# Three score products fewer in a pair's shared tile, and reciprocals carried through a scratch row

## The chip, the cores and the metric

The kernel runs on one core of a Trainium2 chip. The metric is device time of one launch in microseconds (us). TensorE (PE) multiplies matrices and transposes, VectorE (DVE) and ScalarE (ACT) read the products from PSUM, GpSimd (POOL) works on SBUF alone, and SyncE (SP) issues the transfers. Each engine runs its instructions in the order in which the program gives them; they meet by semaphores. There is no scheduler: the kernel's Python code writes the order out by hand.

## The reference

16 heads of attention, then two feed-forward layers:

```python
q_pool = q.reshape(B, H, S // 2, 2, D).mean(axis=3)        # 576 queries of 64 in a head
scores = scale * np.matmul(q_pool, k.transpose(0, 1, 3, 2))  # 576 x 1152
scores = scores - np.max(scores, axis=-1, keepdims=True)
attn = np.exp(scores)
attn = attn / (np.sum(attn, axis=-1, keepdims=True) + 1e-09)
out = np.matmul(attn, v)
...
x = moe(x, w_in, w_out)           # ELU between two products
x = moe2(x, w_gate, w_val, w_out, rms_g)   # RMS norm, SiLU gate, product
```

With B = 2, H = 8, S = 1152, D = 64 there are 16 heads. Everything is float32.

## The kernel before, in words

**Precision.** Products run in a rounded float32 format. A matrix is split into a rounded part (hi) and what the rounding left (lo), and a product is the sum of hi x hi, hi x lo and lo x hi. For scores, `kd` holds the keys' hi in partitions 0 to 63 and their lo in 64 to 127 (`prep_k`). `qt` holds the queries' hi twice, in both halves (u = 0), and their lo (u = 1). One stationary block of queries times `kd` sums 128 partitions at once: hi x hi and hi x lo with u = 0, lo x hi (and lo x lo) with u = 1.

**Pairs and tiles.** Heads go in 8 pairs p; j = 0, 1 is the head within a pair. A head's 576 queries are four tiles of 128 and a rest of 64. The two rests share the ninth tile, M (`i == M`, index 2): the stationary block of each head is padded with zero columns, so that rows 0 to 63 of the result come from one head and rows 64 to 127 from the other. For all other tiles a score tile of 128 x 1152 takes 6 matmuls of 384 columns (2 parts x 3 banks, line 350); M takes 4 parts, so 12.

**Steps.** The attention runs in 72 steps, 9 a pair. Here S0 to S8 name the step by its place in its pair. In a step TensorE does the scores of this tile (`emit_S`), 9 transposes of the exponentials of the tile two steps back (`emit_T`, line 368; LT = 2), and about 8 products with the values (`do_AV`, line 394). In between, VectorE scales the scores, takes the row extremum (line 354), and forms the lo parts of the transposes (line 70); ScalarE does the exponential (line 359) and the hi parts (line 376). A score tile's three banks exist once, so the next scores wait for line 354. The transposes rotate over three banks. Before `emit_T` overwrites a buffer of transposes, `do_T` makes TensorE finish the value products that still read it. In pair 0 the tiles come in the order 0, 1, 3, 4, M, 5, 6, 7, 8 and M is S4; in the other pairs they come in the order of their indices and M is S2.

**Preparation.** GpSimd splits queries, keys and values for the next pair, one job a step, by the table `plan`; `prep_q`, `prep_k` and `prep_v` do it. In pair 0 the first head's jobs are spread over three engines, and head j = 0's queries are prepared by GpSimd in two column ranges, 512 to 576 first (these are M's), then 0 to 512. SP loads the raw arrays one job ahead (`fetch`).

**Row sums.** After a pair's last tile, `emit_r` takes 1/(row sum + 1e-9) for the 9 tiles, a 128 x 9 array, and GpSimd spreads 8 of its columns to 512. `emit_scale` transposes this by 4 matmuls in S6 of the next pair (line 433) and the ninth column by one in S7 (line 438), ScalarE copies them into `xs` (lines 435, 441), and `emit_x` multiplies the pair's output by `xs` on GpSimd. In steps where this is due, the transposes of `emit_T` come behind the value products. The last pair (p = 7) has its own, quicker ending on VectorE and ScalarE.

After attention come the two feed-forward layers, which the change doesn't touch.

Of the kernel before, what the change touches and what calls it, by code (L numbers as in the profile page):

```python
# [39 lines left out]
def tile_kernel(ctx: ExitStack, tc: tile.TileContext, qd, kd, vd, w1d, w2d, wgd, wvd, wod, rgd, outd):  # L40
# [377 lines left out]
    def emit_r(p):  # L418
        s = st[p]
        V.tensor_scalar(out=s[:, 2], in0=s[:, 1], scalar1=1e-9, scalar2=None, op0=ALU.add)  # L420
        V.reciprocal(s[:, 3], s[:, 2])
        rs[p] = ap.tile([128, 640], F32, tag="xs", name="rs", bufs=1)[:, 0:512].rearrange("p (a b) -> p a b", a=8)
        hi_pool(rs[p], s[:, 3, 0:8].to_broadcast([128, 8, 64]))
# [63 lines left out]
    plan = {1: lambda p: ("v", p, 0), 2: lambda p: ("q", p + 1, 1), 3: lambda p: ("k", p + 1, 1, 0),  # L487
            4: lambda p: ("k", p + 1, 1, 1), 5: lambda p: ("v", p + 1, 1), 6: lambda p: ("q", p + 1, 0),
            7: lambda p: ("k", p + 1, 0, 0), 8: lambda p: ("k", p + 1, 0, 1)}
    steps = [(p, i) for p in range(8) for i in ([0, 1, 3, 4, 2, 5, 6, 7, 8] if p == 0 else range(NPT))]  # L490
    ns = len(steps)
    jobs = {n: [] for n in range(-1, ns)}
    for n in range(ns):
# [4 lines left out]
        if k in plan and not (p == 0 and k == 1):  # L498
# [81 lines left out]
    for step in range(ns):  # L580
        emit_S(*steps[step])
# [6 lines left out]
        if step >= LT and not due:  # L588
# [6 lines left out]
        if step >= LT and due:  # L595
            do_T(step)
# [507 lines left out]
```

## Time and profile before

| what | value |
|---|---|
| time of three runs | 667.54, 668.39, 668.79 us; median 668.39 us |
| profiled execution, first to last instruction (span) | 666.8 us |
| the profiled execution's own time | not given with the profile; the median of the runs is 1.6 us over its span |
| TensorE busy | 659.0 us, 99% of the span |
| attention | about the first 250 us |
| VectorE, ScalarE, GpSimd busy over the span | 511.5, 465.2, 443.6 us |
| granted TensorE clock | full in all 40 slices |

Busy shares are means over stages. In attention three engines stand near their limit at once, so the stage is read pair by pair and step by step, with what each engine waits for. Matmuls overlap in the records: the time that one adds is the distance between starts, or its piece in the chain of waits, not its duration.

### The profile page before, as it was taken

Reading aid. Unit: us, or ns where it says so; the run is one execution under the profiler, and the core shown is the slowest. Engines: PE = TensorE matmul, PEld = TensorE weight load, DVE = VectorE, ACT = ScalarE, POOL = GpSimd, SP = SyncE. Lnnn points to the kernel's source line nnn. Section 1 sums busy time; section 2 is a strip of 40 time slices with the busy share of each in tenths; the row PEclk is TensorE's granted clock in tenths of the full one; section 3 lists DMA queues with packets and bytes.
Section 4 is the critical chain, followed back from the end, with each engine's and each line's share of the span. In section 5 each row is a group of like instructions: output and inputs, shape, how many; then the busy total and the mean of one; then the engine's idle time right before and its main releaser. Section 6 shows DMA issues by size and latency. Waiting matters only on the chain.

```text
span 666.8 us, 11391 instructions
## 1 busy us (share of the span) xinstructions
PE 659.0 (99%) x4149; PEld 652.1 (98%) x4149; DVE 511.5 (77%) x884; ACT 465.2 (70%) x910; POOL 443.6 (67%) x407
## 2 busy tenths in 40 slices
PE   7999999999999999999999999999999999999997
PEld 6999999999999999999999999999999999999997
DVE  7989898998999878987786787688697786676200
ACT  6988888898988977848758668866766654564300
POOL 4999888989989323758776695665998874404200
PEclk9999999999999999999999999999999999999999
DMA  6432333233223101142141232110323322204100
GB/s 177 171 107 90 108 131 133 90 108 121 90 89 94 46 1 64 43 148 95 64 158 65 94 129 94 65 64 32 126 96 125 129 94 68 91 1 162 68 36 36
DMA packets 21624, 61.75 MB, mean 93 GB/s; under 512 B 2752, under 2 KB 5056, under 8 KB 21568
## 3 DMA queue, kind: packets, MB, share of 16 engines
q1 hardware_dynamic: 21568, 61.03, 27.9%
q8 instruction: 32, 0.52, 0.3%
q14 instruction: 24, 0.20, 0.1%
HBM read 58.66 MB, written 2.36 MB: 92 GB/s over the span
## 4 chain that ended last, share of the span: by engine, by line
PE 96%; POOL 1%; DVE 1%; DMA 1%; issue 0%; SPq 0%; ACT 0%; POOLq 0%; ACTq 0%
PE b L747 17%; PE b L217 14%; PE b L219 14%; PE b L218 14%; PE s L350 12%; PE o L394 11%; PE t L368 10%; DMA rawq<-in_q_dram 1%; PE t L433 1%; DVE p L354 0%; POOL kd L64 0%; POOL qt L64 0%; PE fb L217 0%; PE fb L219 0%; PE fb L218 0%
## 5 line engine op out<-in xcount | busy, mean ns | idle before, releaser
L64 POOL TENSOR_TENSOR wl<-wt,wh 128x512 fp32r<-128x512 f32 x68 | 91.1, 1340 | 83.9 <-ACT wh L184 79.0
L70 DVE TENSOR_TENSOR ptl<-t,pth 128x384 fp32r<-128x384 f32 x216 | 106.7, 549 | 4.9 <-ACT pth L376 4.5
L354 DVE TENSOR_SCALAR_CACHE_REDUCE p<-s 128x1152 f32<-128x1152 f32 x72 | 97.4, 1354 | 15.1 <-PE s L350 13.7
L376 ACT CAST pth<-t 128x384 fp32r<-128x384 f32 x216 | 89.2, 488 | 22.3 <-PE t L368 21.6
L350 PE MATMUL s<-kd,qt 128*128 128x384 f32 x480 | 98.7, 342 | 2.9 <-DVE p L354 1.4
L359 ACT ACTIVATE p<-p,st 128x1152 f32<-128x1152 f32 x72 | 91.5, 1271 | 0.5 <-DVE p L354 0.2
L217 PE MATMUL b<-xh,wh 128*128 128x384 f32 x260 | 87.7, 337 | 0.0
L350 PEld LDWEIGHTS s<-kd,qt 128*128 128x128 f32 x480 | 81.0, 188 | 6.6 <-DVE p L354 2.8
L219 PE MATMUL b<-xh,wl 128*128 128x384 f32 x260 | 87.5, 336 | 0.0
L218 PE MATMUL b<-xl,wh 128*128 128x384 f32 x260 | 87.4, 336 | 0.0
L394 PE MATMUL o<-pth,vd 128*128 128x256 f32 (+1 forms) x288 | 84.4, 315 | 0.0
L368 PE MATMUL t<-ident,p 128*128 128x128 f32 x648 | 82.5, 272 | 0.0
L394 PE MATMUL o<-ptl,vd 128*128 128x256 f32 (+1 forms) x288 | 78.6, 295 | 0.0
L368 PEld LDWEIGHTS t<-ident,p 128*128 128x128 f32 x648 | 75.0, 141 | 1.8
L120 ACT ACTIVATE we<-wr 128x512 uint32<-128x512 uint32 x68 | 45.4, 667 | 38.8 <-DMA wr<-in_w_dram 19.1
L131 DVE TENSOR_SCALAR wm<-wm 128x512 f32<-128x512 f32 x63 | 43.8, 695 | 20.3 <-ACT wm L122 20.3
L394 PEld LDWEIGHTS o<-pth,vd 128*128 128x128 f32 x288 | 54.3, 189 | 0.3
L122 ACT ACTIVATE wm<-wr 128x512 f32<-128x512 f32 x63 | 39.6, 628 | 21.4 <-DVE wt L136 21.3
L394 PEld LDWEIGHTS o<-ptl,vd 128*128 128x128 f32 x288 | 54.5, 189 | 0.0
L218 PEld LDWEIGHTS b<-xl,wh 128*128 128x128 f32 x260 | 48.8, 188 | 0.0
L217 PEld LDWEIGHTS b<-xh,wh 128*128 128x128 f32 x260 | 48.8, 188 | 0.0
L219 PEld LDWEIGHTS b<-xh,wl 128*128 128x128 f32 x260 | 48.8, 188 | 0.0
(198 smaller groups left out, 1750.6 us busy)
## 6 DMA issues: line engine op xcount, KB each, us to landing
wr<-in_w_dram SPq DMA_DIRECT2D x32, 512.0 KB, 3.2
rawq<-in_q_dram SPq DMA_DIRECT2D x15, 576.0 KB, 4.0
rawk<-in_k_dram SPq DMA_DIRECT2D x28, 288.0 KB, 2.9
wr<-in_wg_dram SPq DMA_DIRECT2D x12, 512.0 KB, 3.2
wr<-in_wv_dram SPq DMA_DIRECT2D x12, 512.0 KB, 3.2
wr<-in_wo_dram SPq DMA_DIRECT2D x12, 512.0 KB, 3.2
rawv<-in_v_dram SPq DMA_DIRECT2D x16, 288.0 KB, 2.9
out_dram<-o SPq DMA_DIRECT2D x12, 192.0 KB, 1.8
```

The lines of the kernel that those rows point to most:

```text
L64: G.tensor_tensor(out=o, in0=i, in1=f(h), op=ALU.subtract)
L70: V.tensor_tensor(out=o, in0=i, in1=f(h), op=ALU.subtract)
L217: PE.matmul(out, lhsT=wh[:, k, :], rhs=ah, start=first and k == 0, stop=False)
L218: PE.matmul(out, lhsT=wh[:, k, :], rhs=al, start=False, stop=False)
L219: PE.matmul(out, lhsT=wl[:, k, :], rhs=ah, start=False, stop=last and k == 3)
L350: PE.matmul(s[:, m, 0:384], lhsT=a, rhs=b[:, 384 * m:384 * m + 384], start=n == 0, stop=n == len(parts) - 1)
L354: V.tensor_scalar(out=pt, in0=s[:, :, 0:384], scalar1=-0.0625, scalar2=None, op0=ALU.mult, op1=ALU.min, accum_out=st[p][:, 0, TILES[i][4], :])
L359: T.activation(out=pt, in_=pt, func=AF.Exp, scale=-1.0, bias=st[p][:, 0, TILES[i][4], :], accum_out=st[p][:, 1, TILES[i][4], :])
L368: PE.transpose(ps[:, k, :], src[:, 128 * b:128 * b + 128], ident)
L376: T.copy(oh, re(ps))
L394: PE.matmul(self.o[:, 0:self.N], lhsT=v[:, b, :], rhs=(pth, ptl)[u][:, g["buf"], b, g["c0"]:320], start=self.n == 0, stop=self.n == 17)
L747: PE.matmul(out, lhsT=a[x][:, k, :], rhs=b[y][:, k, :], start=first and (k, x, y) == (0, 0, 0), stop=last and (k, x, y) == (1, 1, 0), skip ...
```

## The change

M now takes 3 parts: the hi of each head's queries against `kd`, as before, and one product for both heads' lo. For it `bds` is a block-diagonal 128 x 128 array: 64 columns of lo of head 0 in one corner, of head 1 in the other (the rest stays zero). Its moving operand `zd` holds the keys' hi of both heads, stacked in the two halves of the partitions; two transfers a pair copy them there from `kd` (`stack_k`). The queries' hi and lo become separate tiles, and the lo of the last 64 queries is written to `bds` instead of `ql`.

One over the row sums is written into the first nine columns of a 128 x 128 array `rc`, transposed by one matmul (`rows_of_r`, one step after `emit_r`), copied back by ScalarE as 9 rows, stored by five transfers to a row in DRAM (`store_r`, one step later) and read back by two transfers, broadcast over 64 partitions each (`load_r`, one step later). The last pair keeps the old way.

M is S4 in every pair. The jobs for values move: head 1's values in S1 of their own pair and head 0's in S5, with two buffers instead of three. The transposes of `emit_T` always come before the value products.

```diff
+    qt = [(ap.tile([128, 704], F32R, name=f"qh{i}", tag=f"qh{i}"), ap.tile([128, QS], F32R, name=f"ql{i}", tag=f"ql{i}"))
+          for i in range(3)]
+    bds = [ap.tile([128, 128], F32R, name=f"bd{i}", tag=f"bd{i}") for i in range(2)]
...
+    for z in bds:
+        G.memset(f(z), 0.0)
...
+    rc = ap.tile([128, 128], F32, name="rc")
+    G.memset(rc, 1.0)
...
         if (p, j) not in QD:
             QD[p, j] = qt[len(QD) % 3]
-        d, qp = QD[p, j], t[:, 0, :]
+        (h, l), qp = QD[p, j], t[:, 0, :]
+        m, r, o = (0, slice(0, 64), 64) if j else (512, slice(64, 128), 0)
         for a, b in cols:
             (V if hi is hi_dve else G).tensor_tensor(out=qp[:, a:b], in0=qp[:, a:b], in1=t[:, 1, a:b], op=ALU.add)
-            h, l = (d[:, u, 64 + a:64 + b] for u in range(2))
-            hi(h, qp[:, a:b])
-            lo(l, qp[:, a:b], h)
+            hi(h[:, 64 + a:64 + b], qp[:, a:b])
+            for a, b in ((a, min(b, 512)),) if m else ((max(a, 64), b),):
+                if a < b:
+                    lo(l[:, a:b], qp[:, a:b], h[:, 64 + a:64 + b])
+        if any(a <= m < b for a, b in cols):
+            lo(bds[p % 2][r, o:o + 64], qp[r, m:m + 64], h[r, 64 + m:128 + m])
+
+    def stack_k(p, j):
+        if p not in ZD:
+            ZD[p] = ap.tile([128, S], F32R, tag="zd", name="zd", bufs=1)
+        SP.dma_start(out=f(ZD[p][64 * (1 - j):64 * (2 - j)]), in_=f(KD[p, j][0:64]))
...
-            parts = [(QD[p, j][:, u, c:c + 128], KD[p, j]) for j, c in ((1, 0), (0, 576)) for u in (0, 1)]
+            parts = [(QD[p, j][0][:, c:c + 128], KD[p, j]) for j, c in ((1, 0), (0, 576))] + [(bds[p % 2], ZD[p])]
...
+        V.reciprocal(rc[:, 0:NPT], s[:, 2].rearrange("p a b -> p (a b)"))
+        later.extend([(step + 1, rows_of_r), (step + 2, lambda: store_r(p)), (step + 3, lambda: load_r(p))])
+
+    def rows_of_r():
+        ps = tbank()[:, 0:128]
+        PE.transpose(ps, rc, ident)
+        T.copy(rc[0:NPT], ps[0:NPT])
+
+    def store_r(p):
+        d = RD[p] = dp.tile([2, QS], F32, tag="rd", name="rd", bufs=2)
+        for j in range(2):
+            for k in range(2):
+                n = j + 4 * k
+                SP.dma_start(out=d[j:j + 1, 320 * k:320 * k + 256].rearrange("p (k c) -> (p k) c", k=2), in_=rc[n:n + 3:2, :])
+        SP.dma_start(out=d[:, 256:320], in_=rc[8:9, :].rearrange("p (j c) -> p j c", j=2))
+
+    def load_r(p):
+        d = RD.pop(p)
+        xs = XS[p] = ap.tile([128, 640], F32, tag="xs", name="xs", bufs=1)
+        for j in range(2):
+            SP.dma_start(out=xs[64 * j:64 * j + 64, 0:QS], in_=d[j:j + 1, :].to_broadcast([64, QS]))
...
-    plan = {1: lambda p: ("v", p, 0), 2: lambda p: ("q", p + 1, 1), 3: lambda p: ("k", p + 1, 1, 0),
-            4: lambda p: ("k", p + 1, 1, 1), 5: lambda p: ("v", p + 1, 1), 6: lambda p: ("q", p + 1, 0),
+    plan = {1: lambda p: ("v", p, 1), 2: lambda p: ("q", p + 1, 1), 3: lambda p: ("k", p + 1, 1, 0),
+            4: lambda p: ("k", p + 1, 1, 1), 5: lambda p: ("v", p, 0), 6: lambda p: ("q", p + 1, 0),
             7: lambda p: ("k", p + 1, 0, 0), 8: lambda p: ("k", p + 1, 0, 1)}
-    steps = [(p, i) for p in range(8) for i in ([0, 1, 3, 4, 2, 5, 6, 7, 8] if p == 0 else range(NPT))]
+    steps = [(p, i) for p in range(8) for i in (0, 1, 3, 4, 2, 5, 6, 7, 8)]
...
-        do_AV(8, lambda p: later.extend([(step + 2, lambda: emit_scale(p, (0,))),
-                                        (step + 3, lambda: emit_x(p, emit_scale(p, (1,))))]), done)
+        do_AV(8, lambda p: later.append((step + 3, lambda: emit_x(p, XS[p]))), done)
...
+        for u in jobs.get(step - 2, []):
+            if u[0] == "k" and u[3] == 1:
+                stack_k(u[1], u[2])
```

How instructions move is shown at three places. First GpSimd in pair 0, from the second key split on (kd, rawk, vd and rawv are keys and values; qt_92, or qh_93 and ql_94, are head 0's queries, rawq their raw array). Before:

```order
L61 TENSOR_SCALAR kd<-rawk_121 64x576
L64 TENSOR_TENSOR kd<-rawk_121,kd 64x576
L307 TENSOR_TENSOR rawq<-rawq 128x64
L61 TENSOR_SCALAR qt_92<-rawq 128x64
L64 TENSOR_TENSOR qt_92<-rawq,qt_92 128x64
L307 TENSOR_TENSOR rawq<-rawq 128x512
L61 TENSOR_SCALAR qt_92<-rawq 128x512
L64 TENSOR_TENSOR qt_92<-rawq,qt_92 128x512
L64 TENSOR_TENSOR vd<-rawv,vd 128x9x64
```

The same stretch of GpSimd now (bd_97 is `bds[0]`):

```order
L61 TENSOR_SCALAR kd<-rawk_132 64x576
L64 TENSOR_TENSOR kd<-rawk_132,kd 64x576
L314 TENSOR_TENSOR rawq<-rawq 128x64
L61 TENSOR_SCALAR qh_93<-rawq 128x64
L314 TENSOR_TENSOR rawq<-rawq 128x512
L61 TENSOR_SCALAR qh_93<-rawq 128x512
L64 TENSOR_TENSOR ql_94<-rawq,qh_93 128x512
L64 TENSOR_TENSOR bd_97<-rawq,qh_93 64x64
L64 TENSOR_TENSOR vd<-rawv,vd 128x9x64
```

The lo of M's 64 queries moved from ahead of the three 512-column operations to behind them.

Second, TensorE at M (s are scores, t transposes, o value products, p exponentials). Before, S2 of pair 1:

```order
L350 MATMUL s<-kd,qt_92 128x384 x6
L350 MATMUL s<-kd,qt_93 128x384 x6
L394 MATMUL o<-pth,vd 128x320
L394 MATMUL o<-ptl,vd 128x320
L368 MATMUL t<-ident,p 128x128 x9
```

Now, S4 of pair 1:

```order
L369 MATMUL s<-kd,qh_95 128x384 x3
L369 MATMUL s<-kd,qh_91 128x384 x3
L369 MATMUL s<-zd,bd_97 128x384 x3
L413 MATMUL o<-pth,vd 128x256
L413 MATMUL o<-ptl,vd 128x256
L387 MATMUL t<-ident,p 128x128 x9
```

The twelve score products are nine, the last three of them with zd and bds.

Third, TensorE in S6 of a pair, to the scores of S7 (rs are the spread reciprocals). Before:

```order
L350 MATMUL s<-kd,qt_91 128x384 x6
L433 MATMUL t<-ident,rs 128x128 x4
L394 MATMUL o<-pth,vd 128x256
L394 MATMUL o<-ptl,vd 128x256
L394 MATMUL o<-pth,vd 128x256
L394 MATMUL o<-ptl,vd 128x256
L368 MATMUL t<-ident,p 128x128 x9
```

Now:

```order
L369 MATMUL s<-kd,qh_91 128x384 x3
L369 MATMUL s<-kd,ql_92 128x384 x3
L387 MATMUL t<-ident,p 128x128 x9
L413 MATMUL o<-pth,vd 128x256
L413 MATMUL o<-ptl,vd 128x256
```

The four transposes of rs are gone, the transposes of p moved ahead of the value products, and of those two are left instead of four.

## Rows read from the trace of the kernel before

**Rows 1.** The page: span, busy time of the engines, granted clock.
```profile
span 666.8 us, 11391 instructions
...
PE 659.0 (99%) x4149; PEld 652.1 (98%) x4149; DVE 511.5 (77%) x884; ACT 465.2 (70%) x910; POOL 443.6 (67%) x407
...
PEclk9999999999999999999999999999999999999999
```

**Rows 2.** Busy time by pair, M's start to M's start, five pairs.
```profile
core 0: us, PE busy (x) PEld busy (x) DVE busy (x) ACT busy (x) POOL busy (x), PEclk, DMA share, GB/s
129.05:158.73 29.68, 29.68 (x219) 29.20 (x219) 27.14 (x52) 25.54 (x55) 25.01 (x24) 1.00 0.28 91
...
sum 148.71, PE 148.71 PEld 146.08 DVE 136.57 ACT 130.96 POOL 131.26; mean PE 29.74 PEld 29.22 DVE 27.31 ACT 26.19 POOL 26.25
```

**Rows 3.** Waits in that pair: who waits for whom, us, times, longest.
```profile
DVE p L354 <- PE s L350: 2.0, 5, 0.6
```

**Rows 4.** Chain of waits in that pair: start, us added, what.
```profile
129.05 2.11 PE s L350 x12
...
142.29 1.05 PE s L350 x6
143.34 0.44 PE t L433 x4
143.78 0.48 PE o L394 x4
...
148.56 1.28 PE s L350 x6
```

**Rows 5.** TensorE in order of time: starts of S5, S6, S7 in pair 0.
```profile
20.05 1.21 PE L350 MATMUL s<-kd,qt 128*128 128x384 f32 x6
...
23.02 1.21 PE L350 MATMUL s<-kd,qt 128*128 128x384 f32 x6
...
25.17 0.28 PE L394 MATMUL o<-ptl,vd 128*128 128x256 f32 x1
25.69 0.62 PE L350 MATMUL s<-kd,qt 128*128 128x384 f32 x2 [0.24 <-DVE p L354]
```

**Rows 6.** TensorE in order of time: S2 of pair 1, within it a wait.
```profile
38.97 1.41 PE L350 MATMUL s<-kd,qt 128*128 128x384 f32 x7
40.81 0.44 PE L350 MATMUL s<-kd,qt 128*128 128x384 f32 x1 [0.43 <-POOL kd L64]
```

**Rows 7.** TensorE in order of time: starts of S5 and of the next S2.
```profile
139.16 0.34 PE L350 MATMUL s<-kd,qt 128*128 128x384 f32 x1
...
158.56 0.34 PE L350 MATMUL s<-kd,qt 128*128 128x384 f32 x1
```

**Rows 8.** Chain of waits at M of pair 0.
```profile
15.97 2.33 PE s L350 x12
18.30 0.98 PE t L368 x9
```

**Rows 9.** GpSimd in order of time at M of pair 0.
```profile
13.23 0.67 POOL L61 TENSOR_SCALAR kd<-rawk 64x576 fp32r<-64x576 f32 x1
...
16.21 0.32 POOL L64 TENSOR_TENSOR qt<-rawq,qt 128x64 fp32r<-128x64 f32 x1
16.49 1.30 POOL L307 TENSOR_TENSOR rawq<-rawq 128x512 f32<-128x512 f32 x1
17.88 1.01 POOL L61 TENSOR_SCALAR qt<-rawq 128x512 fp32r<-128x512 f32 x1
18.97 1.29 POOL L64 TENSOR_TENSOR qt<-rawq,qt 128x512 fp32r<-128x512 f32 x1
```

**Rows 10.** GpSimd in order of time: the last key split for the next pair.
```profile
157.70 1.43 POOL L64 TENSOR_TENSOR kd<-rawk,kd 64x576 fp32r<-64x576 f32 x1
```

**Rows 11.** Transfers by line: KB each, median us from issue to landing.
```profile
rawk<-in_k_dram SPq DMA_DIRECT2D x28, 288.0 KB, 2.9
...
rawq<-in_q_dram SPq DMA_DIRECT2D x1, 256.0 KB, 5.2
```

**Rows 12.** Groups by line in the first 240 us: the spreading of the reciprocals.
```profile
L61 POOL TENSOR_SCALAR rs<-st 128x512 f32<-128x512 f32 x7 | 5.0, 713 | 5.9 <-DVE st L421 5.8
...
L435 ACT COPY xs<-t 128x512 f32<-128x512 f32 x7 | 4.1, 589 | 3.2 <-PE t L433 3.0
L441 ACT COPY xs<-t 64x64 f32<-64x64 f32 x14 | 2.9, 206 | 0.2
```

More of the change, by code (lines that the diff above doesn't have):

```diff
@@ L275, in tile_kernel @@
     make_identity(nc, ident)
-    for z in qt:
-        V.memset(f(z[:, :, 0:64]), 0.0)
-        V.memset(f(z[:, :, 640:704]), 0.0)
+    for z, _ in qt:
+        V.memset(f(z[:, 0:64]), 0.0)
+        V.memset(f(z[:, 640:704]), 0.0)
+    for z in bds:
+        G.memset(f(z), 0.0)
     V.memset(ones, 1.0)
+    rc = ap.tile([128, 128], F32, name="rc")
+    G.memset(rc, 1.0)
     KD, VD, QD = {}, {}, {}
@@ L340, in emit_S @@
         if i == M:
-            parts = [(QD[p, j][:, u, c:c + 128], KD[p, j]) for j, c in ((1, 0), (0, 576)) for u in (0, 1)]
+            parts = [(QD[p, j][0][:, c:c + 128], KD[p, j]) for j, c in ((1, 0), (0, 576))] + [(bds[p % 2], ZD[p])]
         else:
             j, c, _, _, _ = TILES[i]
-            parts = [(QD[p, j][:, u, c:c + 128], KD[p, j]) for u in (0, 1)]
+            parts = [(QD[p, j][u][:, c - 64 * u:c - 64 * u + 128], KD[p, j]) for u in (0, 1)]
         first = (p, i) == (0, 0)
@@ L420, in emit_r @@
         V.tensor_scalar(out=s[:, 2], in0=s[:, 1], scalar1=1e-9, scalar2=None, op0=ALU.add)
[L421 to L423 removed]
+        if p == 7:
+            V.reciprocal(s[:, 3], s[:, 2])
+            rs[p] = ap.tile([128, 640], F32, tag="xs", name="rs", bufs=1)[:, 0:512].rearrange("p (a b) -> p a b", a=8)
+            hi_pool(rs[p], s[:, 3, 0:8].to_broadcast([128, 8, 64]))
+            return
+        V.reciprocal(rc[:, 0:NPT], s[:, 2].rearrange("p a b -> p (a b)"))
+        later.extend([(step + 1, rows_of_r), (step + 2, lambda: store_r(p)), (step + 3, lambda: load_r(p))])
+    RD = {}
+    def rows_of_r():
[14 more added lines that the diff above has]
+            SP.dma_start(out=xs[64 * j:64 * j + 64, 0:QS], in_=d[j:j + 1, :].to_broadcast([64, QS]))
     XS = {}
@@ L497, in tile_kernel @@
             jobs[n] = u + jobs[n]
-        if k in plan and not (p == 0 and k == 1):
+        if k in plan and not (p == 0 and k in (1, 5)):
             u = plan[k](p)
@@ L580, in tile_kernel @@
     for step in range(ns):
+        if step == 3:
+            stack_k(0, 1)
+            stack_k(0, 0)
         emit_S(*steps[step])
@@ L587, in tile_kernel @@
         due, done = [w for w in later if w[0] <= step], []
-        if step >= LT and not due:
+        rows = [w for w in due if w[1] is rows_of_r]
+        due = [w for w in due if w[1] is not rows_of_r]
+        if step >= LT:
             do_T(step)
@@ L592, in tile_kernel @@
             w[1]()
-        do_AV(8, lambda p: later.extend([(step + 2, lambda: emit_scale(p, (0,))),
-                                        (step + 3, lambda: emit_x(p, emit_scale(p, (1,))))]), done)
-        if step >= LT and due:
-            do_T(step)
+        do_AV(8, lambda p: later.append((step + 3, lambda: emit_x(p, XS[p]))), done)
         for w in done:
@@ L601, in tile_kernel @@
         emit_exp(*steps[step])
+        for w in rows:
+            later.remove(w)
+            w[1]()
         if step >= LT:
```

5 lines of the change are left out of this document (3 added, 2 removed).

## The prediction

> **What bounds the kernel now.** I read the page first. TensorE is busy for 659.0 of 666.8 us at full granted clock [rows 1], so time can go only where TensorE does less or stops waiting; what other engines lose or gain counts through TensorE's waits alone. The windows by pair come next. In attention a pair takes 29.74 us, TensorE is busy for all of it, and VectorE for 27.31, ScalarE for 26.19 and GpSimd for 26.25 [rows 2]. So TensorE bounds, but VectorE is 8% behind it, and its largest wait in a pair is 2.0 us for scores [rows 3]: a shorter TensorE step can soon meet VectorE. Therefore the steps have to be looked at singly, by the chain of waits [rows 4] and by the starts of the scores in the timeline [rows 5 to 7].
>
> **The change in a steady pair (pairs 1 to 7).**
>
> *M's products.* Twelve add 2.11 us to the chain, six 1.05 [rows 4], so three fewer give (2.11 - 1.05)/2 = 0.53 us.
>
> *Transposes of the reciprocals.* Four add 0.44 us [rows 4], 0.11 each. Five become one: -0.44 us.
>
> *A wait that goes.* The scores at 148.56 add 1.28 us where others add 1.05 [rows 4]. VectorE was late there: in the step before, the transposes of p stood behind the value products. They no longer do: -0.23 us.
>
> *A wait that comes.* M as S4 leaves only two value products for S6, where four and the reciprocals' transposes stand now [rows 4]. TensorE is through with S6 before VectorE has read its scores, and the next scores need their banks. Pair 0 already has this order. In its S6 the last value product starts at 25.17 and the next scores at 25.69 [rows 5]; a product of this width adds 0.12 (four add 0.48, [rows 4]), so TensorE stands 0.40 us. From 23.02 to 25.69 are 2.67 us; with S7's slower first products the loss is about 0.53.
>
> Sum: -0.53 - 0.44 - 0.23 + 0.53 = -0.67 us a pair. A second way gives the same. From S5 to the next S2, six steps, pair 0 takes 38.97 - 20.05 = 18.92 us [rows 5, 6] and a pair with the old order 158.56 - 139.16 = 19.40 [rows 7]: -0.48. The other three steps get three score products less (-0.53), one transpose (+0.11) and two value products that S6 lost (+0.24): -0.18. Together -0.66. **Seven pairs give 7 x 0.66 = 4.6 us less.**
>
> What hides the rest: VectorE's work doesn't change. ScalarE loses 0.59 + 2 x 0.21 us a pair and GpSimd 0.71 [rows 12]; ScalarE gains a copy of nine rows, in cost near the 0.21 of the 64 x 64 copy, and GpSimd two 64 x 64 operations, at most the 0.32 of 128 x 64 each [rows 9], against 64 columns less in the two big ones. Both had over 3 us to spare in a pair. The store and reload of the reciprocals begin at S3 and are wanted at S7, four steps of some 3 us; two transfers one after the other, at 2.9 to 5.2 us each [rows 11], fit. SP issues them between loads of raw arrays. The key load behind the stores is delayed by them, but GpSimd prepares for scores that come about three steps later. `zd` needs head 0's keys: their split ends at 157.70 + 1.43 = 159.13 [rows 10]. S2 starts at 158.56 [rows 7], and with S2 and S3 at 3.4 and 3.0 us, M's third part is due near 166.0: 6.9 us for a transfer of 288 KB that takes 2.9 in the nearest row and 5.2 in the slowest [rows 11]. So no cost there; both ends of these rows give zero.
>
> **The change in pair 0.** Here the order of tiles stays, but the lo of M's last 64 queries now comes after all of head 0's other queries on GpSimd. The 64-column lo at 16.21 goes, worth 16.49 - 16.21 = 0.28 us, so the 512-column lo ends at 18.97 + 1.29 - 0.28 = 19.98 [rows 9]. Then comes `bds`, 64 x 64: no row has it, and I take the 0.32 of 128 x 64 (its lower bound is zero, its upper the 1.29 of the 512 columns; the row with the same columns is the nearest). With 0.07 ahead of it, as between such rows, it ends at 20.37. M's third part starts then and takes 0.53, and the transposes behind it start at 20.94 instead of 18.30 [rows 8]: **+2.64 us**. TensorE's queue behind this wait holds those transposes, eight value products and all later scores, and VectorE and ScalarE wait for them, so nothing fills the gap. TensorE stands from 15.97 + 1.05 = 17.02 to 20.4, some 3.4 us, the longest idle time of the program. `zd` doesn't decide here: the last hi of the keys ends at 13.90 [rows 9], and a landing after 2.9 to 5.2 us is at 17 to 19.5.
>
> Afterwards nothing regains it, as TensorE is the bound from 18.30 on. But the wait of 0.43 us for keys in S2 of pair 1 [rows 6] goes: M comes two steps later there, and the values' job of 2.1 us (0.67 + 1.43, like a key split) no longer stands ahead of these keys. -0.43 us.
>
> **Sum:** -4.6 + 2.64 - 0.43 = -2.4 us. On the profiled span that is 666.8 - 2.4 = 664.4; the median of the runs shown lies 1.6 over the span, so **666.0 us**.
>
> [...] The granted clock is full in every slice, the short waits of the first steps included [rows 1]; no row has a gap of 3.4 us. [...]
>
> **Rivals.**
>
> *The clock falls in the gap of pair 0.* For it: a gap unlike any here. Against: the array worked until 17.02, and the waits that there are cost no clock. At half clock the products take twice their time; if that lasts as long as the gap, 3.4 us, it costs 1.7 (3.4 us hold half the work) up to 3.4. 667.7 to 669.4 us. Chance 0.12.
>
> *VectorE takes the bound's place* (the other side). Its 27.3 us of work and its gaps between instructions leave little in 29.7, and M's step, where it now catches up, gets shorter; if its lateness in S6 carries into S7 and S8, the pair stays at 29.74 and all seven pairs give nothing. Then +2.64 - 0.43 = +2.2 us: 670.6. It decides if a pair gains under 0.3 us. Against: pair 0 runs the new order and in S7 and S8 no longer waits. Chance 0.12.
>
> *`zd` or the raw loads come late in every pair*, because SP, in order, waits for splits and for the stored row. Each us beyond the 6.9 costs 7 us in all; a landing after 8 us gives 666.0 + 7.7 = 674. Against: no row over 5.2. Chance 0.05.
>
> *The wait in pair 0 is much smaller than worked out*, if `bds` is ready earlier than I read from the order: without it 666.0 - 2.6 = 663.4. Chance 0.10.
>
> **How the numbers follow.** The forecast has 0.61. A difference of 0.2%, 1.3 us, is what the measurement can tell from no change: faster is under 667.1, slower over 669.7. Within the forecast a pair's gain may be 0.5 to 0.85 (7 x 0.17 = 1.2 us each way) and the start 0.3 off, so 664.7 to 667.3, of which four fifths are faster. Faster: 0.61 x 0.8 + 0.10 = 0.59. Same: 0.12 + most of the clock rival and a part of VectorE's = 0.28. Slower: 0.13. The range goes down to the rival without the gap, 663.4, and up to the clock rival's end, 669.4; outside are VectorE's full price and late transfers.
>
> **What would show it.** Right: 456 score products where there were 480, and 12 transposes of reciprocals (one for each of seven pairs, five for the last) where there were 40; a wait of over 3 us of TensorE near 17 to 20.4 us for `bds` on GpSimd; S6 ending in a wait of about 0.4 us for VectorE; a pair of 29.1 us; no wait of the scores for `zd`. Wrong: a pair still of 29.7 us, a granted clock under 1.00 after the gap, or a TensorE wait for a transfer in M.

## The result and the profile after

The change made the kernel **slower: 673.30 us median of 4 runs (671.52 to 675.61) against 668.19 us of 4 (667.54 to 668.79), ratio 1.0081 [1.0066, 1.0096]**. Forecast were 666.0 us, in a range of 663.4 to 669.4. The profiled execution took 673.91 us, its span is 5.0 us longer than before. The profiled execution of the first run in experiment 2 (1082.56 us) and the one of experiment 12 (802.41 us) ran at a mean granted clock of 0.558 and 0.754, and neither enters any comparison below.

The page of the kernel after, the lines that answer to [rows 1]:

```profile
span 671.8 us, 11405 instructions
...
PE 655.5 (98%) x4097; PEld 647.4 (96%) x4097; DVE 513.1 (76%) x884; ACT 461.4 (69%) x896; POOL 442.5 (66%) x417
...
PEclk9899999999999999999999999999999999999999
```

The work went as planned: 52 matmuls fewer, which are 3 x 8 score products and 4 x 7 transposes. TensorE is busy for less time and the span is longer, so it stands idle more. And the second slice is no longer at full clock.

Busy time by pair, M's start to M's start, answering to [rows 2]:

```profile
core 0: us, PE busy (x) PEld busy (x) DVE busy (x) ACT busy (x) POOL busy (x), PEclk, DMA share, GB/s
49.20:79.85 30.65, 28.99 (x213) 28.36 (x212) 28.27 (x51) 25.09 (x53) 26.40 (x27) 1.00 0.42 127
79.85:109.28 29.43, 29.00 (x213) 28.34 (x212) 27.25 (x51) 25.62 (x54) 24.28 (x25) 1.00 0.50 150
109.28:139.34 30.06, 29.03 (x214) 28.40 (x212) 27.64 (x52) 26.07 (x55) 27.35 (x28) 1.00 0.44 129
...
sum 149.61, PE 144.97 PEld 141.73 DVE 138.02 ACT 128.48 POOL 130.36; mean PE 28.99 PEld 28.35 DVE 27.60 ACT 25.70 POOL 26.07
```

A pair takes 29.92 us on average (149.61 / 5) where 29.07 was forecast and 29.74 was before. TensorE's busy time did fall to 28.99; it now waits 0.4 us in some pairs and 1.0 to 1.7 us in others. TensorE's waits from 36 to 245 us (who waits for whom: us in total, times, longest), where before there was only that of [rows 6]:

```profile
PE t L453 <- DVE ptl L70: 3.0, 3, 1.4
PE s L369 <- DVE p L373: 1.7, 7, 0.2
PE t L387 <- ACT rc L454: 0.6, 3, 0.2
```

The second line is the wait in S6 that was forecast. In the other two the instruction that waits, or the one waited for, belongs to the one transposition that the change adds. The 5.0 us, by the starts of score products in the two timelines and by ScalarE's last copy:

| stretch | before | after | difference |
|---|---|---|---|
| to S2 of pair 1 | 38.97 | 42.46 | +3.49 |
| from there to S8 of pair 7 | 198.98 | 198.70 | -0.28 |
| from there to ScalarE's last copy | 425.40 | 426.14 | +0.74 |
| from there to the end of the span | 3.45 | 4.50 | +1.05 |

The second row should have read -5.0 us (4.6 and 0.43). So there is a start that cost 0.9 us more than forecast (1.2 more from M on: M began 0.34 us earlier than before, at 15.63), a gain in the pairs that didn't arrive, and 1.8 us behind attention that no step had.

**Pair 0.** M's step takes 7.40 us and the next one 3.47, where 4.08 and 2.97 were before. TensorE at M, in order of time (start, us, what, then the idle time before it and its releaser):

```profile
15.63 1.30 PE L369 MATMUL s<-kd,qh 128*128 128x384 f32 x6 [0.70 <-DVE p L373]
19.39 0.79 PE L369 MATMUL s<-zd,bd 128*128 128x384 f32 x3 [2.47 <-POOL bd L64]
20.02 1.50 PE L387 MATMUL t<-ident,p 128*128 128x128 f32 x9
...
21.75 0.41 PE L413 MATMUL o<-pth,vd 128*128 128x256 f32 x1
21.96 0.41 PE L413 MATMUL o<-ptl,vd 128*128 128x256 f32 x1
```

GpSimd there, answering to [rows 9]:

```profile
16.38 0.62 POOL L61 TENSOR_SCALAR qh<-rawq 128x512 fp32r<-128x512 f32 x1
17.08 1.86 POOL L64 TENSOR_TENSOR ql<-rawq,qh 128x512 fp32r<-128x512 f32 x1
19.02 0.32 POOL L64 TENSOR_TENSOR bd<-rawq,qh 64x64 fp32r<-64x64 f32 x1
```

The wait is the one that was forecast, with its name and its cause: the block's lo stands behind 512 columns. Its price, 0.32 us, is the one taken. Behind the gap the value products come 0.21 us apart instead of 0.12. The windows there, with the granted clock behind the busy times:

```profile
20.00:20.50 0.50, 0.50 (x7) 0.47 (x5) 0.28 (x1) 0.00 (x0) 0.50 (x1) 1.00 0.17 60
20.50:21.00 0.50, 0.50 (x6) 0.50 (x4) 0.50 (x1) 0.45 (x2) 0.50 (x2) 0.67 0.12 33
21.00:24.00 3.00, 3.00 (x15) 3.00 (x14) 1.99 (x5) 2.13 (x5) 2.83 (x3) 0.50 0.70 238
24.00:24.50 0.50, 0.50 (x4) 0.50 (x4) 0.00 (x0) 0.00 (x0) 0.50 (x2) 0.92 1.20 328
```

The granted clock is 0.50 from about 20.7 to 24.1 us, after 2.47 us of idling and 1.3 us of work at full clock. That is the first rival.

**S2 of pairs 2, 4 and 6** takes 4.95, 4.33 and 4.37 us, in the odd pairs 3.3. TensorE in S2 of pair 2, from its scores to those of S3:

```profile
71.84 0.70 PE L369 MATMUL s<-kd,qh 128*128 128x384 f32 x3
...
75.01 0.28 PE L413 MATMUL o<-ptl,vd 128*128 128x256 f32 x1
76.71 0.33 PE L453 MATMUL t<-ident,rc 128*128 128x128 f32 x1 [1.42 <-DVE ptl L70]
76.79 0.78 PE L369 MATMUL s<-kd,qh 128*128 128x384 f32 x3
```

The transposition of `rc` takes the next of the three rotating banks, and that is the one that VectorE empties last (`ptl`, line 70). VectorE at that place, then GpSimd:

```profile
72.92 0.21 DVE L445 RECIPROCAL rc<-st 128x9 f32<-128x9 f32 x1
73.05 1.86 DVE L133 SCALAR_TENSOR_TENSOR wt<-wt,we 128x512 uint32<-128x512 uint32 x1
74.83 1.35 DVE L373 TENSOR_SCALAR_CACHE_REDUCE p<-s 128x1152 f32<-128x1152 f32 x1
```
```profile
72.19 0.67 POOL L61 TENSOR_SCALAR vd<-rawv 128x576 fp32r<-128x576 f32 x1
72.94 1.42 POOL L64 TENSOR_TENSOR vd<-rawv,vd 128x576 fp32r<-128x576 f32 x1
```

The same place in the kernel before, which isn't among the rows ahead of the prediction:

```profile
70.29 0.21 DVE L421 RECIPROCAL st<-st 128x9 f32<-128x9 f32 x1
70.42 0.63 DVE L133 SCALAR_TENSOR_TENSOR wt<-wt,we 128x512 uint32<-128x512 uint32 x1
71.68 1.36 DVE L354 TENSOR_SCALAR_CACHE_REDUCE p<-s 128x1152 f32<-128x1152 f32 x1 [0.63 <-PE s L350]
```
```profile
70.69 0.84 POOL L61 TENSOR_SCALAR rs<-st 128x512 f32<-128x512 f32 x1 [1.28 <-DVE st L421]
71.49 0.67 POOL L61 TENSOR_SCALAR vd<-rawv 128x576 fp32r<-128x576 f32 x1
72.25 1.43 POOL L64 TENSOR_TENSOR vd<-rawv,vd 128x576 fp32r<-128x576 f32 x1
```

Line 133 combines a weight for the feed-forward layer, one operation on VectorE in S1 of these three pairs. Before, GpSimd's next job was to spread the reciprocals, and it waited 1.28 us for VectorE to make them; line 133 followed them on VectorE and ran in 0.63 us. After, nothing makes GpSimd wait, the split of the values starts earlier, and line 133 takes 1.86 us: GpSimd's operation ends at 72.94 + 1.42 = 74.36, line 133 at 74.91, 0.55 us later. That is a little under the 0.63 to 0.69 us that it takes when no GpSimd operation is running at its start, as if it had stood until the other engine was through. In pairs 4 and 6 it takes 1.10 us: the shorter operation of that split (0.67 us) had started just before it. The same holds in all fourteen traces that are compared here. In their first 245 us, line 133 and its sister, line 136 (the same operation and shape, in S0 of pairs 3, 5 and 7), run 94 times: 24 times no GpSimd operation is running when they start, and they take 0.63 to 0.69 us; 70 times one is, and they end 0.54 to 0.66 us after it, whether that makes 0.68 or 1.93 us. Why it would stand, the traces don't show.

**S3 of the odd pairs** takes 3.39 to 3.46 us instead of 2.97 to 3.06. TensorE, then ScalarE in S3 of pair 3:

```profile
106.97 0.82 PE L387 MATMUL t<-ident,p 128*128 128x128 f32 x6
107.98 0.55 PE L387 MATMUL t<-ident,p 128*128 128x128 f32 x3 [0.19 <-ACT rc L454]
```
```profile
106.43 1.25 ACT L378 ACTIVATE p<-p,st 128x1152 f32<-128x1152 f32 x1
107.68 0.24 ACT L454 COPY rc<-t 9x128 f32<-9x128 f32 x1
```

The nine transposes of a step go to the three rotating banks, three to each. One is held by the transposition of `rc` until ScalarE copies it, and this copy stands behind the exponential of S2. The third group waits for it.

### The profile page after: what moved, and what is told of

It is laid out like the page before. It is cut to its first block, busy times and chain, and to the rows that moved or that the text cites. A ratio compares the mean times of both kernels' runs of the same rounds, so it can differ in the third digit from the quotient of the medians.

```text
span 671.8 us, 11405 instructions
## 1 busy us (share of the span) xinstructions
PE 655.5 (98%) x4097; PEld 647.4 (96%) x4097; DVE 513.1 (76%) x884; ACT 461.4 (69%) x896; POOL 442.5 (66%) x417
## 4 chain that ended last, share of the span: by engine, by line
PE 51%; ACT 1%; DVE 1%; issue 0%; ACTq 0%; DVEq 0%
PE b L801 16%; PE b L217 12%; PE b L219 12%; PE b L218 12%; DVE eg L249 0%; PE b L769 0%; ACT eg L247 0%; PE b L779 0%; ACT gh L250 0%; DVE wt L136 0%; ACT wm L122 0%; ACT wh L184 0%; ACT eg L248 0%; ACT o L1099 0%; DVE u L842 0%
## 5 line engine op out<-in xcount | busy, mean ns | idle before, releaser
L120 ACT ACTIVATE we<-wr 128x512 uint32<-128x512 uint32 x68 | 45.5, 668 | 40.5 <-DMA wr<-in_w_dram 20.7
L369 PE MATMUL s<-kd,qh 128*128 128x384 f32 x240 | 57.1, 350 | 3.4 <-DVE p L373 3.4
L122 ACT ACTIVATE wm<-wr 128x512 f32<-128x512 f32 x63 | 39.6, 628 | 20.8 <-DVE wt L136 20.6
L217 PE MATMUL b<-gh,wh 128*128 128x384 f32 x144 | 48.4, 336 | 0.0
```

The lines of the kernel that those rows point to most:

```text
L217: PE.matmul(out, lhsT=wh[:, k, :], rhs=ah, start=first and k == 0, stop=False)
L369: PE.matmul(s[:, m, 0:384], lhsT=a, rhs=b[:, 384 * m:384 * m + 384], start=n == 0, stop=n == len(parts) - 1)
```

## The experiments

There are fourteen runs, of twelve kernels. Unless said otherwise an edit is made on the changed kernel. Times are medians, ratios are against the kernel before on the same chip (667.8 to 668.2 us). Differences to the changed kernel go across chips, so 0.4 us of them can be the chip's.

**1. The block's lo early.** In pair 0 GpSimd writes the block right behind M's hi, ahead of the 512 columns.

```diff
             hi(h[:, 64 + a:64 + b], qp[:, a:b])
+            if a <= m < b and len(cols) > 1:
+                lo(bds[p % 2][r, o:o + 64], qp[r, m:m + 64], h[r, 64 + m:128 + m])
...
-        if any(a <= m < b for a, b in cols):
+        if len(cols) == 1 and any(a <= m < b for a, b in cols):
```

> Only the place of one instruction changes: in pair 0 the lo of M's last 64 queries is written to bds right after their hi, ahead of the 512-column operations on GpSimd. Theory A (the start costs 2.5 us of wait and about 1.3 us of half clock after it, since the granted clock of the changed kernel is 0.50 from 20.7 to 24 us): M's step in pair 0 falls from 7.40 us to under 4.3, the next from 3.47 to 2.97, the clock is 1.00 throughout attention, and the median falls by 3.5 to 4 us, from 673.3 to about 669.5. Rival B (the clock falls for another reason, such as the transfers of zd): the wait goes, the half clock stays, and the median falls by about 2.5 us, to 670.8. Rival C (zd itself arrives late behind the first wait): M's third product waits for a transfer, and less than 1.5 us is gained.

Measured: 669.41 us (667.31 to 670.11), ratio 1.0017 [1.0008, 1.0025], 3.9 us less than the changed kernel. M's step takes 3.76 us, the next 3.05, the clock stays full. S2 of pairs 2, 4 and 6 (5.18, 4.15 and 4.35 us) and S3 of the odd pairs (3.39 to 3.46) stay long. The start is a loss of its own, of 3.9 us.

**2 and 11. TensorE kept busy in the gap.** Twenty transpositions that nobody reads stand ahead of M's third part in pair 0.

```diff
+            if (p, i, m, n) == (0, M, 0, 2):
+                warming(20)
             a, b = parts[n]
```

> The changed kernel with 20 transposes of the identity, whose result nobody reads, between the second and the third part of M in pair 0; they add nothing to the computation and take about 2.1 of the 2.47 us in which TensorE waits for bds. Theory A (the clock falls because TensorE is idle): the wait for bds shrinks to some 0.4 us, bds is ready at the same time, the granted clock stays at 1.00, and the steps after M get 1.3 to 1.5 us shorter (transposes 0.90 instead of 1.16, eight value products 0.94 instead of 1.7, next scores 1.05 instead of 1.5): median about 672. Rival B (contention or another reason): the clock of 0.50 from 20.7 to 24 us stays and so does the median of 673.3.

Measured: 671.70 us (670.82 to 673.62, five executions), ratio 1.0060 [1.0048, 1.0072], so 1.6 us less. The trace is that of the second run:

> The twenty transpositions in TensorE's gap of pair 0 once more, for a look at the granted clock (the trace of the first such run can't be used). Theory A (half clock after the gap comes from TensorE's idling): granted clock 1.00 from 20 to 25 us, the value products behind M 0.12 us apart instead of 0.21, M's step and the next 1.5 us shorter together (9.4 instead of 10.9 us); about 671.8 us. Rival B (the clock falls for another reason): 0.50 from about 21 to 24 us again.

Measured: 672.0 us, one run. The windows of that trace:

```profile
20.50:21.00 0.50, 0.50 (x7) 0.50 (x6) 0.43 (x1) 0.10 (x1) 0.50 (x1) 1.00 0.00 0
21.00:22.00 1.00, 1.00 (x11) 1.00 (x10) 1.00 (x3) 1.00 (x3) 1.00 (x2) 1.00 0.00 0
```

The clock stays full, so it fell because TensorE idled (theory A). M's step and the next take 6.57 + 2.95 = 9.52 us instead of 7.40 + 3.47 = 10.87. So the clock cost at least 1.35 us of pair 0, and the wait, net of the three products saved, 9.52 - (4.08 + 2.97) = 2.47 us at most, where 2.64 was forecast. Here M's third part starts 4.00 us after M and in the changed kernel 3.76, which moves up to 0.24 us from the wait to the clock.

**3. The row's transposition later and at the front of S3.** Its store and reload come one step later too.

```diff
-        later.extend([(step + 1, rows_of_r), (step + 2, lambda: store_r(p)), (step + 3, lambda: load_r(p))])
+        later.extend([(step + 2, rows_of_r), (step + 3, lambda: store_r(p)), (step + 4, lambda: load_r(p))])
...
+        for w in rows:
+            later.remove(w)
+            w[1]()
         if step >= LT:
             do_T(step)
```

> The changed kernel with the transpose of the reciprocals and ScalarE's copy of it one step later and ahead of that step's other transposes, where its bank has been read long before. Theory A (the transpose waits for the bank that VectorE empties last, and the next step's transposes wait for ScalarE's late copy): in pairs 1, 3, 5, 7 S3 falls from 3.45 to about 3.0 us, in pairs 2, 4, 6 S2 falls by 0.5 of its 4.4 to 5.0 us, the rest of that step being VectorE's own lateness; together 4 x 0.45 + 3 x 0.5 = 3.3 us, median about 670. Rival B (VectorE is late anyway, and the transpose only shows it): S2 of the pairs 2, 4, 6 stays over 4.3 us, only the odd pairs gain, 1.5 us. Rival C (the whole wait of S2 in the even pairs is the transpose's): 4 x 0.45 + 3 x 1.3 = 5.7 us, median 667.6.

Measured: 684.27 us, ratio 1.0243 [1.0225, 1.0260]: 11 us slower than the changed kernel, which no theory had. S3 of pairs 1, 3 and 5 doesn't fall either (3.49, 4.04 and 4.05 us), and S2 of pairs 2 and 4 stays at 4.27 and 4.37 us, near what rival B has, with no transposition of the row in it; in pair 6 it is 3.52. TensorE's S2 of pair 2, from its scores to those of S3:

```profile
73.24 0.70 PE L369 MATMUL s<-kd,qh 128*128 128x384 f32 x3
...
77.51 0.80 PE L369 MATMUL s<-kd,qh 128*128 128x384 f32 x3 [0.82 <-DVE p L373]
```

Line 133 takes 1.85 us in that pair and VectorE reads the scores late, so TensorE waits for the scores' banks where it waited for the transposition's. The 11 us have another cause. TensorE's waits, then its place at M of pair 3 and GpSimd's ahead of it:

```profile
PE s L369 <- DMA zd<-kd: 7.0, 3, 3.2
```
```profile
114.38 1.33 PE L369 MATMUL s<-zd,bd 128*128 128x384 f32 x3 [2.50 <-DMA zd<-kd]
```
```profile
93.66 1.43 POOL L314 TENSOR_TENSOR rawq<-rawq 128x576 f32<-128x576 f32 x1 [2.36 <-DMA rawq<-in_q_dram]
```

SP's issues stand one behind another. In pair 2 the load of these queries was issued at 87.95 us, behind a load of values that stood until 85.97 (GpSimd's key split, which frees its buffer, ended at 85.94) and behind the reload's two issues (1.5 us); in the changed kernel it was issued at 84.03. So GpSimd waited for its queries, split the keys late, and `zd` was issued at 105.30 us behind three other loads. It is not shown which of these delays is the reload's own. The third rival (`zd` late) is real, one step away. And half clock came again behind the waits of 2.50 us (0.50 from 114.5 to 117) and 3.17 us (value products at 180.65 and 180.87 us, 0.22 apart). In pair 0 the same start cost 1.2 us more than in the changed kernel: after a gap of 2.46 us the clock was at 0.50 for 6.8 us (18.8 to 25.6) instead of 3.4.

**4. VectorE's weight operation behind S3** in pairs 2, 4 and 6 (a table entry each).

```diff
-(2, 1): 1, ... (4, 1): 1, ... (6, 1): 1
+(2, 4): 1, ... (4, 4): 1, ... (6, 4): 1
```

> The changed kernel with one VectorE operation of the weight stream (line 133), which in pairs 2, 4 and 6 stands between the last work of S1 and the scores of S2, moved behind S3, where M's longer scores follow. Theory A (VectorE, made late by this operation of 1.1 to 1.9 us, keeps TensorE waiting in S2 of these pairs): S2 falls from 4.95, 4.33 and 4.37 us to the 3.3 of the other pairs, 3.7 us in all, of which the odd pairs' wait for ScalarE's copy (0.45 us in S3) comes back: net 2.4 us, median about 671. Rival B (the transpose waits for its bank in any case): S2 stays over 4 us. Rival C (the wait moves to M's step): S2 falls but S4 grows from 3.7 by over 0.5 us in these pairs, and the net is under 1 us.

Measured: 671.78 us (670.36 to 673.87), ratio 1.0061 [1.0049, 1.0074], 1.5 us less. S2 there falls to 3.32, 3.49 and 3.38 us, but S3 there rises from 3.06 to between 3.27 and 3.45: with S2 short, ScalarE's copy is late in S3 of these pairs too.

**5. Both, 1 and 4.**

> The block's lo parts early in pair 0 as in the first experiment, and VectorE's weight operation (L133) of pairs 2, 4 and 6 behind S3 instead of in S1. Theory A (the losses are separate places and add up): the first gave 3.9 us, the second 1.5 us, so 673.3 - 5.4 = 667.9 us, with M's step of pair 0 near 3.8 us and S2 of pairs 2, 4 and 6 near 3.4 us; S3 of the odd pairs stays at 3.45 us. Rival B (what is taken away in S2 is waited for later in the pair, because VectorE is the bound there): 669 to 670 us, as the first experiment alone.

Measured: 666.97 us (665.59 to 669.20), ratio 0.9992 [0.9983, 1.0001]. The gains add up, and this is no different from the kernel before. S3 stays at 3.3 to 3.46 us in five of seven pairs.

**6. And ScalarE's copy of the row ahead of its exponential.**

```diff
-        emit_exp(*steps[step])
         for w in rows:
             later.remove(w)
             w[1]()
+        emit_exp(*steps[step])
```

> As the one before, and ScalarE's copy of the row of inverses stands ahead of its exponential of the same step instead of behind it. Theory A (in S3 TensorE waits for the bank which that copy frees): S3 goes from 3.45 to about 3.0 us in the pairs where it is long, four times or more, so 1.8 to 3 us less than the one before: 665 to 666 us. Rival B (the copy is short of nothing but TensorE's own transposition, or VectorE is late in S3 anyway): within 0.5 us of the one before, 667.5 to 668.4 us.

Measured: **664.98 us (664.65 to 665.71), ratio 0.9957 [0.9946, 0.9969]**, the fastest kernel of this study. S3 takes 3.05 to 3.07 us in every pair, and of TensorE's waits from 36 to 234 us one line is left, the forecast one:

```profile
PE s L371 <- DVE p L375: 1.7, 7, 0.2
```

**7. The nine products without the row.** Changed kernel with 1 and with the scaling of before (`emit_r`, `emit_scale`, the place of `emit_T`).

> The nine score products of the shared tile alone (block lo early in pair 0, order and preparation as in the changed kernel), with the scaling of the kernel before: four transpositions of the row sums in S6 and one in S7, no row of inverses, no scratch row. Theory A (VectorE's lateness in S2 is a loss of its own, the transposition of the row another): M's step 0.6 us shorter in seven pairs (-4.3), S2 of pairs 2, 4 and 6 still 1.0 us longer (+3.0), nothing in S3: about 666.5 us, M's step near 3.7 and S2 of pairs 2, 4 and 6 at 4.0 to 4.4 us. Rival B (the row's transposition makes the whole loss in S2 and S3): 663 to 664 us.

Measured: 666.05 us (664.92 to 666.39), ratio 0.9969 [0.9957, 0.9981], near theory A's time but not for its reason. S2 of pairs 4 and 6 takes 3.28 and 3.29 us although line 133 is still in S1; in these it takes 0.63 us, since GpSimd's spreading is back and keeps the split of the values behind it. In pair 2 it takes 1.19 us beside another GpSimd operation and S2 is 3.73. So VectorE's lateness comes from the row's edit, by way of GpSimd, not from the order of tiles. A pair is at 29.1 to 29.2 us where TensorE waits for nothing. There is one wait of 1.71 us for `zd` in pair 5, after which the clock stays at 1.00.

**8. The row without the nine products.** Kernel before with `rows_of_r`, `store_r` and `load_r`.

> The kernel before with its twelve products and its order, and only the scaling changed: one transposition of the row of inverses in S2 (there M's step), a scratch row and a broadcast load, so S6 and S7 lose five transpositions. Theory A (the transposition costs where VectorE is late; beside M's twelve products it is not): S6 and S7 gain 0.5 us a pair, S3 loses up to 0.4 us where the copy comes behind the exponential: 665 to 667 us. Rival B (the transposition and its copy cost as much as in the changed kernel, 0.45 to 1.4 us a pair, wherever they stand): 669 to 671 us.

Measured: 668.26 us (667.54 to 669.05), ratio 1.0005 [0.9996, 1.0014]: A's mechanism, but neither time. S6, S7 and S8 take 2.67, 3.31 and 3.25 us instead of 2.86, 3.53 and 3.31 (0.47 less), and S3 takes 3.45 in six of seven pairs instead of 2.97 (0.48 more). TensorE, then ScalarE in S3 of pair 2:

```profile
73.18 0.27 PE L437 MATMUL t<-ident,rc 128*128 128x128 f32 x1
...
75.36 0.55 PE L371 MATMUL t<-ident,p 128*128 128x128 f32 x3 [0.20 <-ACT rc L438]
```
```profile
73.82 1.25 ACT L362 ACTIVATE p<-p,st 128x1152 f32<-128x1152 f32 x1
75.07 0.24 ACT L438 COPY rc<-t 9x128 f32<-9x128 f32 x1
```

The transposition ran at 73.18, and its copy stood behind the exponential for 1.6 us. Four transposes gone are paid for by one bank held too long. And S0 of pairs 3, 5 and 7 takes 3.99, 3.94 and 3.82 us instead of 3.50 to 3.53: line 136 takes 1.77 to 1.93 us there, as GpSimd's operation (1.43 us) started just before it.

**9. The order of tiles alone,** with the plan of the value splits, on the kernel before: twelve products and old scaling.

> The kernel before with only the order of the tiles in pairs 1 to 7 (M as fifth step) and the plan of the value splits changed: twelve products for M, the scaling of before. Theory A (the order by itself is nearly free; what cost in the changed kernel is the row's transposition and copy, that meet VectorE and ScalarE late): a pair as in the nine products alone (29.10 us) and 0.53 us more for three products, 29.63 us instead of 29.74, and the wait for keys in S2 of pair 1 (0.43) gone: 666.6 to 667.4 us. Rival B (M's long step is missed in S2, where VectorE's weight operation stands): S2 of pairs 2, 4 and 6 1 us longer: 669.5 to 671 us.

Measured: 666.93 us (666.50 to 667.40), ratio 0.9982 [0.9973, 0.9991], theory A. S2 takes 3.28 or 3.29 us in every pair, line 133 takes 0.63, and the kernel is 1.3 us faster; the order costs nothing, and 0.43 us of its gain is the wait of [rows 6].

**10. The copy first alone.**

> The changed kernel with one edit: ScalarE's copy of the row of inverses ahead of its exponential of the same step. Theory A (in S3 TensorE's third group of transpositions waits for the bank that this copy frees): S3 of pairs 1, 3, 5 and 7 goes from 3.45 to 3.05 us; in pairs 2, 4 and 6 the wait of S2 for the bank that VectorE empties (1.0 to 1.4 us) stays, and the start of pair 0 too: 1.6 to 2 us less than 673.3, so 671.3 to 671.7 us. Rival B (the copy comes late because its transposition does): no change, 673 us.

Measured: 672.54 us (672.03 to 673.14), ratio 1.0066 [1.0053, 1.0079]. S3 falls to 3.03 to 3.07 us in every pair as A has it, but the gain is 0.8 us, not 1.6 to 2: S2 of pair 7 rises from 3.41 to 4.25, where the transposition now meets VectorE late as in the even pairs (four such waits instead of three, 3.7 us in all).

**12. The fifth kernel once more,** for a trace of one of its longer runs.

> The fifth kernel again (block's lo early, VectorE's weight operation later), for another execution's trace: its times lay between 665.6 and 669.2 us, far wider than those of the kernel with the copy first (664.7 to 665.7), and the trace at hand is of the shortest. Theory A (in the longer ones transfers that stand in SP's queue behind the late copy come late, zd or raw keys): if this execution is over 667 us, M's third part waits for zd in one or two pairs, 1 us or more each. Rival B (the scatter comes after the attention): the scores of the last step start at 234.0 us again.

Measured: 802.41 us, one execution; it tells nothing.

**13 and 14. The row's transfers on ScalarE's queue,** with the copy late (as in 5) and with the copy first (as in 6).

```diff
-                SP.dma_start(out=d[j:j + 1, ...
+                T.dma_start(out=d[j:j + 1, ...
```

> The fifth kernel (block's lo early, VectorE's weight operation later, copy behind the exponential) with the stores of the row and its reloads issued by ScalarE instead of SP, so that no raw load stands behind them. Theory A (the scatter comes from raw loads and zd that wait in SP's order behind the stores): runs within 1.5 us of each other, median near the shortest of the fifth kernel, 665.6 us (at most 666.2). Rival B (it comes from elsewhere, the copy's own lateness among it): runs over 3 us apart again, median 666.7 to 667.3 us.

> The kernel with the copy first (665.0 us) and the same change of queue. Theory A (with the copy first SP's order costs nothing): 664.7 to 665.3 us. Rival B (SP's order still delays raw loads): 1 us less, 664.0 us. Rival C (ScalarE loses time by issuing seven transfers a pair, and VectorE and TensorE wait for it): over 666 us.

Measured: 700.23 us, ratio 1.0476 [1.0462, 1.0490], and 697.27 us, ratio 1.0438 [1.0421, 1.0456]. Against 5 and 6 they lost 33 and 32 us: rival C of the second, of which only the direction was on record. ScalarE of the first, with its queue's issues (ACTq):

```profile
79.69 2.40 ACTq L464 DMA_DIRECT2D rd<-rc  x4
82.13 0.56 ACTq L465 DMA_DIRECT2D rd<-rc  x1
82.74 1.26 ACT L380 ACTIVATE p<-p,st 128x1152 f32<-128x1152 f32 x1 [2.63 <-DVE wt L133]
...
88.07 0.48 ACTq L471 DMA_DIRECT2D xs<-rd  x1
88.59 0.37 ACT L434 COPY olo<-o 64x256 f32<-64x256 f32 x1 [3.38 <-DMA rawv<-in_v_dram]
```

The five issues of the stores take 3 us, ScalarE computes nothing for 2.63 us before its exponential, and the second reload stands in its queue until 88.07 us, 5.4 us behind the last store's issue; the profile doesn't tell for what. TensorE then stands for 3.2 to 4.0 us in six pairs, and each time the granted clock falls to 0.50 (in this pair from 92.0 to 95.4 us; the mean of the whole execution is 0.983). What the experiment was for, the scatter of the fifth kernel, it can't tell.

## Why the prediction was wrong

**Products (-0.53).** Right: in the same order of tiles M's step takes 4.23 to 4.26 us with twelve products (experiment 9) and 3.71 after, 0.52 to 0.55 less.

**Transposes (-0.44), the wait that goes (-0.23), the wait that comes (+0.53).** Right together. From S5 to the next S2 18.92 us were forecast for the new order; from 172.46 to 191.38 it is 18.92.

**"One transpose (+0.11)" in the other three steps: the step that failed.** S2, S3 and M together were to shrink from 10.27 to 10.09 us. They take 10.46 to 10.50 in the odd pairs and 11.1 to 11.7 in the even ones. The working priced the transposition as TensorE's time and let its bank be free. It has two ends: the bank has to be empty before (VectorE), and stays taken until ScalarE's copy, behind an exponential of 1.25 us. Over what S2 and S3 take where neither end is late (3.32 and 3.05 us), S2 of pairs 2, 4 and 6 lost 3.7 us and S3 of the odd pairs 1.6: 5.3 in all, the whole gain of 4.6 and more. The 3.7 are not the bank's alone. In experiment 3, with no transposition in S2, pair 2 still loses 1.0 us there to VectorE's late read of the scores. Beside the same line 133 (1.85 us in pair 2, 1.10 in pair 6) the bank adds 0.68 and 0.85 us to that (4.95 against 4.27, 4.37 against 3.52). With both ends mended (experiment 6) the same stretch, S2 of pair 1 to S8 of pair 7, takes 194.29 us, 4.69 less than before, against 5.03 forecast.

**"VectorE's work doesn't change."** Wrong in its effect, and the other part of the loss in S2: line 133 grew from 0.63 us to between 1.10 and 1.86, because GpSimd no longer waited for VectorE's reciprocals (0.63 again where it does, in pairs 4 and 6 of experiment 7 and in all three of 9). The trace of before showed that wait (5.9 us in seven pairs, [rows 12]), and I counted only the work that went.

**The start (+2.64).** Right in mechanism, 2.2 to 2.5 us measured, but the clock's 1.35 to 1.6 us on top were given to a rival with 0.12. (By its own terms, 20.37 and 0.53, the sum is 2.60.) I put the gap at 3.4 us idle; 2.47 was enough. The rows of before have only shorter waits, so their full clock said nothing of a longer one and was no ground to give the rival so little. Half clock, twice the time for a product and a stretch as long as the gap were my assumptions there, and no row had them. The trace of after shows 0.50 for 3.4 us behind 2.47 us of idling, and value products 0.21 us apart, 1.8 times the 0.12 of full clock; in experiment 3 nine transposes at 0.50 take 1.77 us to the next product instead of 0.90.

**-0.43 for the keys in S2 of pair 1.** Right: that S2 takes 3.29 us and waits for no keys.

**Rivals.** The clock's came true; it was to end at 669.4 at most, as it was added to pairs that gain. VectorE's "takes the bound's place" has the size (the pairs gained 0.28 us and not 4.6) but not the way: S6 to S8 are short, and VectorE decides in S2 of three pairs alone. `zd` late every pair: not in the changed kernel's trace. Its price was too low all the same: one transfer of the kernel before, of 2 KB, does take over 5.2 us (6.2), and in experiment 7, whose trace has its landings, `zd` took 3.1 to 8.7 us, 5.8 in the median; the 8.7 is the one that M waited for, issued behind three other loads.

**The end (+1.05), which no step had.** The store of the last output lands later after ScalarE's last copy. The trace's packet records show an instruction packet of 8192 bytes at 669.41 us, and the last eight output packets behind it from 669.72 to 670.31; before, the last such packet comes at 662.21 and the outputs land by 665.33. In the traces of experiments 7, 8 and 9 no instruction packet falls between the last copy's end and the landing, and from that copy's start to the end of the span 3.36 to 3.43 us pass; in those of 1, 3, 4, 5, 6, 10 and 11 one does, and it is 3.95 to 4.36. With the row's transfers off SP's queue (13 and 14) the packet is gone from there and the end takes 3.36 us in both. So I infer that the issues which the change adds to SP move a fetch of its instructions into the last store; whose fetch the packet is, no trace shows.

**Open.** The 0.74 us between attention and the last copy: TensorE waits twice for VectorE in the feed-forward part (0.7 us in all), in the changed kernel and in experiment 6, and not in 1 or 5, whose code there is the same. And the scatter: the changed kernel's runs lie 4.1 us apart and those of 1, 4 and 5 2.8 to 3.6, but with the copy first (6 and 10) 1.1, with the nine products alone (7) or the row alone (8) 1.5, and before's 0.9 to 1.6. So it seems to take a late copy and the transfers of `zd` together, as if the stores that wait for the copy sometimes held up what stands behind them on SP; which transfer that is, no trace showed, and with 4 to 12 executions of each this is argued and not shown. Two parts can be named. Where pair 0 has its gap, the time goes with the clock: the six executions of 4 took 670.36 us at a mean granted clock of 0.999, 671.66 to 671.78 at 0.997, 672.45 at 0.995 and 673.87 at 0.994. And in the traces of the changed kernel, 1 and 11, whose code from pair 1 on is the same, S0 of pairs 3, 5 and 7 takes from 3.51 to 3.96 us, the longer the closer line 136 starts behind a GpSimd operation.

## What to carry to other kernels

Price an added operation by what it holds, not by its duration: a transposition of 0.11 us cost 0.4 to 0.85 us a pair, because its bank had to be emptied by one engine before and by another behind a long operation; with both ends early it cost at most 0.3 (S2 of 3.31 to 3.61 us in experiment 6, against 3.28 without it in 9). When work is taken from an engine that waits for another, ask what that engine then does earlier and whom it meets. And a queue carries a delay to what stands behind it: on SP's a load was issued at 87.95 us instead of 84.03 (experiment 3), and with the row's transfers on ScalarE's TensorE stood for 20.6 us in six pairs (experiment 13).

## What the hardware showed that was not expected

- Half clock after 2.47 us of idling (0.50 from 21 to 24 us) and after 2.50 us (experiment 3), and full clock after 1.71 us (experiment 7). After gaps of 2.47 and 2.46 us the half clock lasted 3.4 us in one trace and 6.8 in another (experiment 3).
- VectorE's lines 133 and 136: 0.63 to 0.69 us when no GpSimd operation was running at their start; otherwise they ended 0.54 to 0.66 us after that operation, 70 times out of 70, and took up to 1.93 us.
- An issue of a transfer of 0.5 to 144 KB on ScalarE's queue took 0.47 to 0.61 us of its time, a few 1.1 to 1.2 (experiments 13 and 14); with seven of them and their waits S5 took 6.7 to 7.9 us (experiment 14) instead of 2.97.
- The end took 3.95 to 4.5 us with an instruction packet ahead of the last output packets, and 3.36 to 3.43 without.
